# The opening of a Fourier filter and feed-forward kernel: another order for its loads, folds and turns

## The chip, the cores and the metric

The kernel runs on one core of one Trainium2 chip. The core has five engines that work side by side, each in the order of its own instruction list: TensorE (PE, with PEld for its weight loads), VectorE (DVE), ScalarE (ACT), GpSimd (POOL) and SyncE (SP, which only issues DMAs). Transfers run on 16 DMA engines; here SP and POOL issue them. The metric is the time of one execution on the device in microseconds (us). The kernel before takes 904.9 us, the median of 3 runs (904.34 to 905.48).

## The reference

Two stages follow one another. The first filters each of 256 columns along a sequence of 3008 in the frequency domain; the second is a feed-forward block with a normalisation ahead of it.

```python
def _attn_ref(x, filt_r, filt_i):          # x: 8 x 3008 x 256
    X = np.fft.rfft(x, axis=1)
    Y = X * (filt_r + 1j * filt_i)[None, :, :]
    return np.fft.irfft(Y, n=x.shape[1], axis=1)

def _moe_ref(x, w_gate, w_val, w_out, rms_g):   # x: 24064 x 256, w: 256 x 1536
    rms = np.sqrt(np.mean(x * x, axis=-1, keepdims=True) + 1e-06)
    xn = x / rms * rms_g
    g = xn @ w_gate
    silu = g * (1.0 / (1.0 + np.exp(-g)))
    return silu * (xn @ w_val) @ w_out
```

## The kernel before

The transforms of length 3008 = 47 x 64 are done as matmuls with constant tables, in three steps for each of the eight batches:

- s1: a transform of length 47 (`s1`, L139, one matmul for two of 32 row groups, 16 calls a batch; psum name psa). Its result goes to DRAM (`a_tmp`, one store for four calls) and comes back in another layout in four reads (`load_a2`, L156).
- s2 and s2z: the transform of length 64 (`s2`, psp), the product with the filter, and the way back (`s2z`, psz), 12 calls a batch. The result goes to DRAM (`z_tmp`, one store for three calls) and comes back in another layout (`load_z2`, L240). I call this the z trip.
- s3: the way back over 47 (`s3`, L247, psy), 16 calls a batch, with the sums of squares taken on ScalarE, rho = 1/rms on GpSimd (`s3r`) and the scaling on VectorE (`s3n`). The result goes to DRAM (`n_tmp`) and comes back transposed as `xn`.

The feed-forward block runs in chunks of up to 512 tokens. A unit (`unit`, L337) is one of 12 blocks of 128 of the 1536 inner columns: two matmuls for the gate (pg), two for the value (pv), Silu on ScalarE (sg), the product on VectorE (hh). Its projection (`project`, L354, po) follows three units later (LAG). A chunk's result is copied out of PSUM by ScalarE and VectorE and stored. Batch 0 makes 8 chunks of 376 tokens, every other batch 6; units are counted on through all chunks, so that unit 12 begins the second chunk of batch 0 and unit 96 the first of batch 1.

The order is written by hand (`manual_schedule`): each engine gets its instructions in the order of the calls. From the first unit on, `plan` holds lists of steps by slot: `at(k, f, ...)` puts a step behind the matmuls of unit k, and within a slot s3n, then s3r, then s2z, then all others run (`ORDER`, L430). So batch 0's remaining chunks (from the third, `PRE` = 2), batch 1's s2 and s3 and all of the later batches run between units.

The opening (L492 to L551) is what comes before the first unit. Batch 0 is worked through s1, s2 and s2z without a trip between s1 and s2. Near its end, at j = 10 of the loop at L513, GpSimd issues the four loads of batch 1's x (`load_x(1)`, which cast and so are issued by GpSimd), folds four of the twelve weight stages (`fold_w`: weights times the norm's gain, into their final type) and issues the first third of w_out (`load_wo`). After the last s2z the z trip's reads are issued, with eight rows each of 32 (`load_z2(0, 0, 8)`, `load_z2(0, 8, 8)`), and four more weight stages (`load_w(4)`). Then come 12 of batch 1's 16 s1 calls, s3 of the first two chunks, the last four s1 calls, and the two chunks' scaling and turn: `turn_n` (L294) scales a chunk (`s3n_first`), turns it with eight matmuls (psn) and copies it to `xn`, one half by ScalarE and one by VectorE. Four folds stand between the two turns, four in slot 5.

Buffers that matter: the x tiles, the a tiles have four each; `xn` and the weight stages share nine; PSUM has eight banks; `z2` and `a2` have one buffer each.

Of the kernel before, what the change touches and what calls it, by code (L numbers as in the profile page):

```python
# [74 lines left out]
def kernel(  # L75
# [11 lines left out]
    nc = tc.nc  # L87
# [8 lines left out]
    a_dram = nc.dram_tensor("a_tmp", (B, NS, 4, RP, D), FP16, kind="Internal").ap()  # L96
# [8 lines left out]
    def bank(name):  # L105
        return psum.tile([P, 512], FP32, tag="bank", name=name)
# [15 lines left out]
    PRE = 2  # L122
# [4 lines left out]
    st = [Batch() for _ in range(B)]  # L127


    def load_x(b):  # L130
        v = st[b]
        v.x = []
        for g in range(4):
            xt = work.tile([PX, 8, D], FP16, tag="xt", name="xt", bufs=4)
            nc.gpsimd.dma_start(
                xt, x[b].rearrange("(p r) d -> p r d", r=RP)[:, ds(8 * g, 8), :])
            v.x.append(xt)

    def s1(b, i, eng):  # L139
        v = st[b]  # L140
        if i % 4 == 0:
            v.a = work.tile([QZ, 8, D], FP16, tag="a_sb", name="a_sb", bufs=4)
        ps = bank("psa")
        nc.tensor.matmul(ps[0:QZ, :], w1_sb, v.x[i // 4][:, ds(2 * (i % 4), 2), :],  # L144
                         start=True, stop=True)
        dst = v.a[:, ds(2 * (i % 4), 2), :]
        src = ps[0:QZ, :].rearrange("p (r d) -> p r d", r=2)
        if eng == 0:
            nc.scalar.activation(out=dst, in_=src, func=AXT.Copy)  # L149
        else:  # L150
            nc.vector.tensor_copy(out=dst, in_=src)
        if i % 4 == 3:
            nc.sync.dma_start(
                a_dram[b].rearrange("s c r d -> (s c) r d")[:, ds(8 * (i // 4), 8), :], v.a)

    def load_a2(b):  # L156
        v = st[b]
        v.a2 = work.tile([P, NS, D], FP16, tag="a2", name="a2", bufs=1)
        for cr in range(4):
            nc.sync.dma_start(v.a2[cr:P:4], a_dram[b, :, cr].rearrange("s r d -> r s d"))  # L160
# [79 lines left out]
    def load_z2(b, r0=0, n=RP):  # L240
        v = st[b]
        if r0 == 0:
            v.z2 = work.tile([QZ, RP, D], FP16, tag="z2", name="z2", bufs=1)
        nc.sync.dma_start(v.z2[:, ds(r0, n), :],
                          z_dram[b, ds(r0, n)].rearrange("r c s d -> (c s) r d"))
# [36 lines left out]
    def s3n_first(c):  # L282
        v = st[0]
        n = work.tile([PY, 8, D], FP16, tag="n_sb", name="n0", bufs=2)
        for k in range(2):
            ps, rho = v.y.pop(2 * c + k)
            nc.vector.tensor_tensor(out=n[:, ts(k, 2), :],
                                    in0=ps[0:PY, :].rearrange("p (r d) -> p r d", r=2),
                                    in1=rho.unsqueeze(-1).to_broadcast([PY, 2, D]), op=ALU.mult)
        if c >= PRE:  # L290
            nc.sync.dma_start(n0_dram[c], n[:, 0:4, :])
        return n

    def turn_n(c):  # L294
        n = s3n_first(c)
        xn = work.tile([P, 2, 512], FP16, tag="xn", name="xn", bufs=9)
        for dh in range(2):
            ps = bank("psn")
            for r in range(4):
                nc.tensor.matmul(ps[:, ts(r, PY)], n[:, r, ts(dh, P)], eye_sb[0:PY, 0:PY],  # L300
                                 start=(r == 0), stop=(r == 3))
            dst = xn[:, dh, 0:4 * PY].rearrange("d (p r) -> d r p", r=4)
            src = ps[:, 0:4 * PY].rearrange("d (r p) -> d r p", r=4)
            if dh == 0:
                nc.scalar.activation(out=dst, in_=src, func=AXT.Copy)
            else:
                nc.vector.tensor_copy(out=dst, in_=src)
        st[0].xn[c] = xn
# [12 lines left out]
        st[b].xn[c] = xn  # L321

    for v in st:
        v.t12, v.y, v.xn = {}, {}, {}


    chunks = []
# [69 lines left out]
    def at(slot, f, *args):  # L397
        plan.setdefault(slot, []).append((f, args))

    for c in range(PRE, RP // 4):  # L400
        k = 2 + 8 * (c - PRE)
        at(k, s3, 0, 2 * c, 2)
        at(k + 1, s3, 0, 2 * c + 1, 2)
        at(k + 2, s3r, 0, 2 * c, 2)
        at(k + 4, s3n_first, c)
        at(k + 7, load_xn_first, c)

    for b in range(1, B):
        end = FIRST + UNITS * (b - 1)
        o_s1 = 44 if b == 2 else end - 118  # L410
        o_s2, p_s2 = (12, 3) if b == 1 else (end - 75, 2)
        o_s3 = 62 if b == 1 else end - 31
        if b > 1:
            at(o_s1 - 18, load_x, b)
            for i in range(16):
                at(o_s1 + i, s1, b, i, i % 2 if b == 2 else 0)
            at(o_s1 + 16, load_a2, b)
        for j in range(12):
            k = o_s2 + p_s2 * j
            at(k, s2, b, j)  # L420
            at(k + (3 if b < 2 else 5), s2z, b, j)
        at(k + (4 if b < 2 else 6), load_z2, b)
        for q in range(16):
            k = o_s3 + q + (q // 2 if b == 1 else q // 4)
            at(k, s3, b, q)
            at(k + 1, s3r, b, q)
            at(k + 2, s3n, b, q)
        for c in range(6):
            at(k + 3 + c, load_xn, b, c)
# [46 lines left out]
    def load_w(n):  # L476
        for w_d, w_sb, dt_, k in pieces[len(stages):len(stages) + n]:
            stage = work.tile([P, 512], FP32, tag="xn", name="stage", bufs=9)
            nc.sync.dma_start(stage, w_d[ds(dt_ * P, P), ts(k, 512)])
            stages.append(stage)  # L480

    def fold_w(i, eng):
        w_d, w_sb, dt_, k = pieces[i]
        eng.tensor_scalar(out=w_sb[:, dt_, ts(k, 512)].rearrange("a (i p) -> a i p", i=4),  # L484
                          in0=stages[i].rearrange("a (p i) -> a i p", i=4),
                          scalar1=g_sb[:, ds(dt_, 1)], scalar2=None, op0=ALU.mult)

    def load_wo(k):
        nc.gpsimd.dma_start(wo_sb[:, ts(k, 4), :],
                            moe_w_out.rearrange("(k p i) d -> k p i d", p=P, i=4)[k])  # L490

    with tc.manual_schedule():  # L492
        load_x(0)
        nc.sync.dma_start(w1_sb, w1_d)
        nc.sync.dma_start(u_sb, u_d)
        nc.sync.dma_start(eye_sb, eye_d)
        nc.sync.dma_start(w0_sb, w0_d)
        nc.sync.dma_start(t_sb, t_d)
        for dh in range(2):
            nc.sync.dma_start(g_sb[:, ds(dh, 1)], moe_rms_g[ds(dh * P, P)].unsqueeze(-1))  # L500
        nc.vector.memset(half_sb, -0.5)
        load_f(0, nc.gpsimd)
        for g in range(4):
            s1_first(g)
            if g < 3:
                make_v(2 * g)
                make_v(2 * g + 1)
            if g > 0:

                nc.vector.memset(fr_sb[0:1, 6 * g, 0:1], 0.0)  # L510
                load_f(g, nc.sync)
        copy_f(0)
        for j in range(15):  # L513
            if j < 12:
                turn(j)
            if 0 <= j - 2 < 12:
                s2(0, j - 2)
            if j in (2, 5, 8):
                copy_f(j // 3 + 1)
            if 0 <= j - 4 < 12:  # L520
                s2z(0, j - 4)
            if j == 6:
                load_w(4)
            if j == 10:
                load_x(1)
                for i in range(4):
                    fold_w(i, nc.gpsimd)
                load_wo(0)
        s2z(0, 11)
        load_z2(0, 0, 8)  # L530
        load_z2(0, 8, 8)
        load_w(4)
        for i in range(12):
            s1(1, i, i % 2)
        for c in range(PRE):
            s3(0, 2 * c, 2)
            s3(0, 2 * c + 1, 2)
            s3r(0, 2 * c, 2)
        for i in range(12, 16):
            s1(1, i, 1)  # L540
        load_wo(1)
        load_wo(2)
        turn_n(0)
        load_w(4)
        for i in range(4, 8):
            fold_w(i, nc.vector)
        turn_n(1)
        load_z2(0, 16, 16)
        load_a2(1)
        for i in range(8, 12):  # L550
            at(5, fold_w, i, nc.vector)  # L551

        total = len(chunks) * JT
        for u in range(total + LAG):
            if u < total:
                unit(u // JT, u % JT)
                steps(u)
            if u >= LAG:
                project((u - LAG) // JT, (u - LAG) % JT)
        assert not plan, sorted(plan)  # L560
# [30 lines left out]
```

## Time and profile before

| | us |
|---|---|
| median of 3 runs | 904.9 |
| the profiled execution's own time | 903.57 |
| its span in the profile | 901.7 |
| TensorE busy in the span | 862.3 |
| VectorE busy | 645.6 |
| ScalarE busy | 640.1 |
| GpSimd busy | 336.5 |
| first s3 matmul of batch 0 | 49.28 |
| first unit | 60.97 |
| first s3 matmul of batch 1 | 138.23 |
| first unit of batch 1 (unit 96) | 175.31 |

The page cuts the span into 40 slices of 22.5 us and gives each a digit of busy tenths. A row of the chain of waits is a piece of the chain that ended last: its start, its length, and the instruction or transfer. A row of the timeline gives start, length, engine, line, operation, result<-operands, shapes, and in brackets the idle time before it with what ended it. A row of the windows gives a stretch, its length, the busy time of PE, PEld, DVE, ACT and POOL with the number of instructions, the granted TensorE clock, the DMA share and GB/s.

### The profile page before, as it was taken

How to read it: one execution, taken by the hardware profiler on the slowest of the kernel's cores; microseconds unless marked ns; L12 is line 12 of the kernel's file. 1: busy time of each engine (PE TensorE's matmuls, PEld its weight loads, DVE VectorE, ACT ScalarE, POOL GpSimd, SP SyncE). 2: the span in 40 equal slices, each digit the busy share in tenths (PEclk: the TensorE clock that was granted, in tenths of full speed). 3: DMA queues.
4: the chain of work that ended last, by engine and by line, in shares of the span. 5: the costliest groups of instructions: out<-in, count | busy, mean ns of one | idle time of the engine just before them, and what ended most of it. 6: DMA issues, size and time to landing. Idle time of an engine off the chain costs nothing.

```text
span 901.7 us, 16399 instructions
## 1 busy us (share of the span) xinstructions
PE 862.3 (96%) x5528; PEld 549.6 (61%) x5528; DVE 645.6 (72%) x1025; ACT 640.1 (71%) x1455; POOL 336.5 (37%) x438
## 2 busy tenths in 40 slices
PE   5659999999999999999999999999999999999997
PEld 4326766666556655666556665566656665665655
DVE  4658887895588947697477965789477985865554
ACT  5546678777886778677886878867786775854543
POOL 3712104592245803285044821459033850500000
PEclk9859999999999999999999999999999999999999
DMA  9995766565436565354645554365653425260101
GB/s 211 238 257 124 167 156 212 122 145 130 144 101 143 128 146 170 99 108 129 163 146 129 138 123 151 106 131 145 146 159 100 97 78 117 77 130 24 42 29 45
DMA packets 140796, 117.30 MB, mean 130 GB/s; under 512 B 53960, under 2 KB 125256, under 8 KB 140712
## 3 DMA queue, kind: packets, MB, share of 16 engines
q1 hardware_dynamic: 136472, 102.36, 42.5%
q0 software_dynamic: 4240, 13.90, 8.6%
q8 instruction: 43, 0.70, 0.3%
q14 instruction: 41, 0.34, 0.1%
HBM read 56.96 MB, written 60.42 MB: 130 GB/s over the span
## 4 chain that ended last, share of the span: by engine, by line
PE 87%; ACT 4%; DMA 3%; DVE 2%; issue 2%; POOL 1%; ACTq 0%; SPq 0%; DVEq 0%; POOLq 0%
PE po L364 26%; PE pv L346 26%; PE pg L342 25%; PE psy L250 2%; PE psa L144 2%; ACT junk L256 2%; PE psz L229 2%; PE psp L200 2%; ACT sg L349 2%; DMA fi_sb<-in_filt_i_dram 1%; DMA z_tmp<-z_sb 1%; DMA z<-z_tmp 1%; DVE t L208 1%; DVE hh L351 0%; POOL fi_sb L450 0%
## 5 line engine op out<-in xcount | busy, mean ns | idle before, releaser
L351 DVE TENSOR_TENSOR hh<-pv,sg 128x512 f16<-128x512 f32 (+2 forms) x600 | 392.5, 658 | 219.8 <-ACT sg L349 128.3
L349 ACT ACTIVATE sg<-pg 128x512 f32<-128x512 f32 (+2 forms) x600 | 340.6, 568 | 193.8 <-PE pg L342 159.9
L364 PE MATMUL po<-wo_sb,hh 128*128 128x256 f16 (+2 forms) x2304 | 349.4, 272 | 0.2 <-DVE n_sb L276 0.2
L346 PE MATMUL pv<-xn,wv_sb 128*128 128x512 f16 (+2 forms) x1200 | 342.2, 367 | 4.4 <-ACT sg L349 3.8
L342 PE MATMUL pg<-xn,wg_sb 128*128 128x512 f16 (+2 forms) x1200 | 342.4, 367 | 0.6 <-DVE wg_sb L484 0.3
L364 PEld LDWEIGHTS <-hh 128*128 128x128 f16 (+2 forms) x2304 | 235.0, 104 | 102.4 <-DVE n_sb L276 0.5
L346 PEld LDWEIGHTS <-wv_sb 128*128 128x128 f16 x1200 | 117.5, 98 | 132.7 <-issue 6.3
L265 POOL TENSOR_SCALAR me<-ms 96x2 f32<-96x2 f32 (+1 forms) x120 | 26.0, 217 | 349.3 <-ACT junk L256 348.4
L342 PEld LDWEIGHTS <-wg_sb 128*128 128x128 f16 x1200 | 117.4, 98 | 14.1 <-issue 1.1
L217 POOL TENSOR_TENSOR pi<-pi,fi_sb 64x512 f32<-64x512 f32 x72 | 91.3, 1268 | 70.4 <-ACT pi L214 66.6
L256 ACT ACTIVATE junk<-psy 96x256 f16<-96x256 f32 x256 | 97.1, 379 | 20.9 <-PE psy L250 8.7
L218 POOL TENSOR_TENSOR qq<-pr,pi 128x512 f16<-128x512 f32 x72 | 91.6, 1272 | 10.2 <-DVE pi L216 4.4
L267 POOL TENSOR_TENSOR rho<-me,half_sb 96x2 f32<-96x2 f32 (+1 forms) x120 | 87.3, 728 | 10.0
L276 DVE TENSOR_TENSOR n_sb<-psy,rho 96x512 f16<-96x512 f32 x112 | 75.8, 677 | 0.0
L234 ACT ACTIVATE z_sb<-psz 128x512 f16<-128x512 f32 x96 | 57.3, 597 | 10.1 <-PE psz L232 5.8
L149 ACT ACTIVATE a_sb<-psa 96x512 f16<-96x512 f32 x94 | 55.4, 591 | 7.2 <-PE psa L144 3.5
L250 PE MATMUL psy<-z,t_sb 96*96 96x512 f16 x128 | 49.2, 389 | 7.8 <-DMA z<-z_tmp 7.8
L216 DVE TENSOR_TENSOR pi<-psp,fi_sb 64x512 f32<-64x512 f32 x72 | 49.9, 693 | 1.9
L215 DVE TENSOR_TENSOR pr<-psp,fr_sb 128x512 f32<-128x512 f32 x72 | 49.6, 689 | 0.6
L256 ACT ACTIVATION_READ_ACCUMULATOR junk<-psy 96x1 f32 x256 | 49.0, 191 | 0.0
L214 ACT ACTIVATE pi<-psp 64x512 f32<-64x512 f32 x72 | 42.4, 588 | 6.1
L144 PE MATMUL psa<-xt,w_sb 94*96 94x512 f16 x112 | 42.5, 399 | 3.0 <-DMA xt<-in_x_dram 2.8
(53 smaller groups left out, 382.6 us busy)
## 6 DMA issues: line engine op xcount, KB each, us to landing
out_dram<-o SPq DMA_DIRECT2D x70, 256.0 KB, 2.5
z_tmp<-z_sb SPq DMA_DIRECT2D x32, 384.0 KB, 2.3
xt<-in_x_dram POOLq DMA_DIRECT2D x32, 376.0 KB, 7.3
a_tmp<-a_sb SPq DMA_DIRECT2D x28, 384.0 KB, 3.6
a<-a_tmp SPq DMA_DIRECT2D x28, 384.0 KB, 5.5
z<-z_tmp SPq DMA_DIRECT2D x7, 1536.0 KB, 10.0
n_tmp<-n_sb SPq DMA_DIRECT2D x28, 384.0 KB, 3.0
out_dram<-o SPq DMA_DIRECT2D x14, 224.0 KB, 2.6
```

What stands on the lines that cost most here:

```text
L144: nc.tensor.matmul(ps[0:QZ, :], w1_sb, v.x[i // 4][:, ds(2 * (i % 4), 2), :], start=True, stop=True)
L217: nc.gpsimd.tensor_tensor(out=pi[64:P], in0=pi[64:P], in1=fi[64:P], op=ALU.mult)
L218: nc.gpsimd.tensor_tensor(out=qq, in0=pr, in1=pi, op=ALU.subtract)
L250: nc.tensor.matmul(ps[0:PY, :], t_sb, v.z2[:, ts(q, 2), :], start=True, stop=True)
L256: nc.scalar.activation(out=junk, in_=ps[0:PY, ts(i, D)], func=AXT.Square, scale=0.0625, accum_out=v.ms[:, ds(k + i, 1)])
L267: nc.gpsimd.tensor_tensor(out=rho, in0=me, in1=half_sb[:, 0:2 * pair], op=ALU.pow)
L276: nc.vector.tensor_tensor(out=v.n[:, ds(2 * (q % 4), 2), :], in0=ps[0:PY, :].rearrange("p (r d) -> p r d", r=2), in1=rho.unsqueeze(-1).to_ ...
L342: nc.tensor.matmul(pg[:, 0:w], wg_sb[:, dt_, ts(jt, P)], xn[:, dt_, 0:w], start=(dt_ == 0), stop=(dt_ == 1))
L346: nc.tensor.matmul(pv[:, 0:w], wv_sb[:, dt_, ts(jt, P)], xn[:, dt_, 0:w], start=(dt_ == 0), stop=(dt_ == 1))
L349: nc.scalar.activation(out=sg[:, 0:w], in_=pg[:, 0:w], func=AXT.Silu)
L351: nc.vector.tensor_tensor(out=hh[:, 0:w], in0=pv[:, 0:w], in1=sg[:, 0:w], op=ALU.mult)
L364: nc.tensor.matmul(po[0:n, ts(s4 % 2, D)], hh[:, ds(s4 * wb, n)], wo_sb[:, jt, :], start=(jt == 0 and s4 % 2 == 0), stop=(jt == JT - 1 and ...
```

## The change

The diff is shown whole. It does the following:

- `load_x` takes a list of groups, and batch 1's four groups are loaded in three steps on GpSimd's list: groups 0 and 1, two folds, group 2, two folds, group 3, then the first third of w_out.
- The first two z reads take four rows each instead of eight; rows 8 to 15 are read later, rows 16 to 31 in slot 4, behind the reads of batch 1's a.
- `s1` can hand its stores back (`later`). Only eight s1 calls of batch 1 stand before s3 now, four more stand between s3 of the first and of the second chunk, all on VectorE; the last four are in slots 2 to 4, on ScalarE. The first two a stores follow after s3, then the z read of rows 8 to 15, the last four weight stages, the third a store; the fourth a store and the a reads are in slot 4.
- `turn_n` gets its scaled chunk from outside. Both chunks are scaled before the units, the first is turned there, the second in slot 2.
- The eight folds on VectorE are in slots 0, 1, 4 and 5, two in each.
- In the plan, batch 0's third and later chunks and batch 1's s2 and s2z come four slots later, batch 1's s3 one slot later.

```diff
--- before.py
+++ after.py
@@ -127,16 +127,15 @@
     st = [Batch() for _ in range(B)]
 
 
-    def load_x(b):
-        v = st[b]
-        v.x = []
-        for g in range(4):
+    def load_x(b, groups=range(4)):
+        v = st[b]
+        for g in groups:
             xt = work.tile([PX, 8, D], FP16, tag="xt", name="xt", bufs=4)
             nc.gpsimd.dma_start(
                 xt, x[b].rearrange("(p r) d -> p r d", r=RP)[:, ds(8 * g, 8), :])
             v.x.append(xt)
 
-    def s1(b, i, eng):
+    def s1(b, i, eng, later=None):
         v = st[b]
         if i % 4 == 0:
             v.a = work.tile([QZ, 8, D], FP16, tag="a_sb", name="a_sb", bufs=4)
@@ -150,8 +149,13 @@
         else:
             nc.vector.tensor_copy(out=dst, in_=src)
         if i % 4 == 3:
-            nc.sync.dma_start(
-                a_dram[b].rearrange("s c r d -> (s c) r d")[:, ds(8 * (i // 4), 8), :], v.a)
+            def store(a=v.a):
+                nc.sync.dma_start(
+                    a_dram[b].rearrange("s c r d -> (s c) r d")[:, ds(8 * (i // 4), 8), :], a)
+            if later is None:
+                store()
+            else:
+                later.append(store)
 
     def load_a2(b):
         v = st[b]
@@ -291,8 +295,7 @@
             nc.sync.dma_start(n0_dram[c], n[:, 0:4, :])
         return n
 
-    def turn_n(c):
-        n = s3n_first(c)
+    def turn_n(c, n):
         xn = work.tile([P, 2, 512], FP16, tag="xn", name="xn", bufs=9)
         for dh in range(2):
             ps = bank("psn")
@@ -321,7 +324,7 @@
         st[b].xn[c] = xn
 
     for v in st:
-        v.t12, v.y, v.xn = {}, {}, {}
+        v.x, v.t12, v.y, v.xn = [], {}, {}, {}
 
 
     chunks = []
@@ -398,7 +401,7 @@
         plan.setdefault(slot, []).append((f, args))
 
     for c in range(PRE, RP // 4):
-        k = 2 + 8 * (c - PRE)
+        k = 6 + 8 * (c - PRE)
         at(k, s3, 0, 2 * c, 2)
         at(k + 1, s3, 0, 2 * c + 1, 2)
         at(k + 2, s3r, 0, 2 * c, 2)
@@ -408,8 +411,8 @@
     for b in range(1, B):
         end = FIRST + UNITS * (b - 1)
         o_s1 = 44 if b == 2 else end - 118
-        o_s2, p_s2 = (12, 3) if b == 1 else (end - 75, 2)
-        o_s3 = 62 if b == 1 else end - 31
+        o_s2, p_s2 = (16, 3) if b == 1 else (end - 75, 2)
+        o_s3 = 63 if b == 1 else end - 31
         if b > 1:
             at(o_s1 - 18, load_x, b)
             for i in range(16):
@@ -522,33 +525,45 @@
             if j == 6:
                 load_w(4)
             if j == 10:
-                load_x(1)
-                for i in range(4):
-                    fold_w(i, nc.gpsimd)
-                load_wo(0)
+                load_x(1, (0, 1))
+                fold_w(0, nc.gpsimd)
+                fold_w(1, nc.gpsimd)
         s2z(0, 11)
-        load_z2(0, 0, 8)
-        load_z2(0, 8, 8)
+        load_x(1, (2,))
+        fold_w(2, nc.gpsimd)
+        fold_w(3, nc.gpsimd)
+        load_x(1, (3,))
+        load_wo(0)
+        load_z2(0, 0, 4)
+        load_z2(0, 4, 4)
         load_w(4)
-        for i in range(12):
-            s1(1, i, i % 2)
+        a_stores = []
+        for i in range(8):
+            s1(1, i, i % 2, a_stores)
         for c in range(PRE):
             s3(0, 2 * c, 2)
             s3(0, 2 * c + 1, 2)
             s3r(0, 2 * c, 2)
-        for i in range(12, 16):
-            s1(1, i, 1)
+            if c == 0:
+                for i in range(8, 12):
+                    s1(1, i, 1, a_stores)
+        for f in a_stores[:2]:
+            f()
+        load_z2(0, 8, 8)
+        load_w(4)
+        a_stores[2]()
         load_wo(1)
         load_wo(2)
-        turn_n(0)
-        load_w(4)
-        for i in range(4, 8):
-            fold_w(i, nc.vector)
-        turn_n(1)
-        load_z2(0, 16, 16)
-        load_a2(1)
-        for i in range(8, 12):
-            at(5, fold_w, i, nc.vector)
+        n0 = s3n_first(0)
+        turn_n(0, n0)
+        n1 = s3n_first(1)
+        at(2, turn_n, 1, n1)
+        for i in range(4, 12):
+            at((0, 0, 1, 1, 4, 4, 5, 5)[i - 4], fold_w, i, nc.vector)
+        for i in range(12, 16):
+            at(2 + (i - 11) // 2, s1, 1, i, 0)
+        at(4, load_a2, 1)
+        at(4, load_z2, 0, 16, 16)
 
         total = len(chunks) * JT
         for u in range(total + LAG):
```

## The prediction

> **What bounds the kernel now.** I read the page first, then the chain of waits of the opening, the timeline there, and the timeline around the first place where a later batch leans on the opening. The two strips of the page's second part:
>
> ```profile
> PEclk9859999999999999999999999999999999999999
> DMA  9995766565436565354645554365653425260101
> ```
>
> TensorE is at 9 tenths from the fourth slice on, and the waits after 75 us put only 5 us of TensorE idle time down to anything. So the time is the opening's length plus a nearly full TensorE stream: what counts is how early the feed-forward units start, and holes made later. Only in the first slices is the DMA at 9 while TensorE is not, and TensorE runs there at half clock. The chain of waits of the first 120 us, start and length:
>
> ```profile
> 35.32 7.07 DMA z_tmp<-z_sb
> 42.94 6.29 DMA z<-z_tmp
> 49.28 0.64 PE psy L250
> ...
> 58.02 0.66 DVE wg_sb L484
> 58.68 0.58 DVE wv_sb L484
> 59.26 1.20 DVE n L287 x2
> 60.51 0.66 PE psn L300 x6
> 61.17 0.63 PE pg L342 x2
> ```
>
> The last z store and the first z read are 13.4 us in which TensorE has nothing but four matmuls of s1; then 11.7 us of normalising and turning both chunks, with four folds between, before the first unit (its first matmul at 60.97). I call the first s3 matmul T: 49.28 before. What shares the DMA, by the timeline:
>
> ```profile
> 29.86 2.10 POOL L135 DMA_DIRECT2D xt<-in_x_dram  x4
> 32.12 2.07 POOL L484 TENSOR_SCALAR wg_sb<-stage,g_sb 128x512 f16<-128x512 f32 x1 [0.15 <-issue]
> 40.20 0.62 POOL L489 DMA_DIRECT2D wo_sb<-in_moe_w_out_dram  x1
> 42.55 1.13 SPq L244 DMA_DIRECT2D z<-z_tmp  x2
> 58.04 10.97 SPq L160 DMA_DIRECT2D a<-a_tmp  x4
> ```
>
> The four x loads land 5.2, 6.7, 8.5 and 10.7 us after their issues (35.05, 37.05, 39.4, 42.1): one group per 2.35 us. The last z store, issued with groups two to four still moving, lands after 7.1; the first, issued at 24.70 before them, after 3.5.
>
> **The change, part by part. (1) x in three steps.** POOL issues groups 0 and 1 (29.86 plus two issues of 0.53), folds twice (2.04 each), issues group 2 at 35.0, folds twice, issues group 3 at 39.6 and the first wo load at 40.2, as before. The last z store still shares with group 2, but not with group 3: 7.1 - 2.35 = 4.75, landing at 40.05 instead of 42.4. Gain 2.35; bounds 0 and 3.6 (down to 3.5). s1 of groups 0 to 2 stays hidden under the trip; group 3 lands at some 44, ten us before its matmuls among the units.
>
> **(2) The first read halved.** 192 instead of 384 KB before T. A 1536 KB read of this kind lands in a median 10.0 us, so 192 KB is worth about 1.0. Against it, group 3 is now issued just when the read is: a whole group is 2.35, nothing is the other end. I take 0.8, as the two queues take turns and the wo load was beside the read before too. So T' = 49.28 - 2.35 - 1.0 + 0.8 = 46.7, gain 2.55 (bounds 0 and 4.9).
>
> The Trainium skill (DMA: Bandwidth & Descriptors, Queues, rings and completion order) says each DMA engine goes round-robin, packet by packet, between the queues with work; by that rule alone group 3 takes its whole 2.35 out of the read, T' is 48.3, and the sum below loses 1.5. The 7.1 against 3.5 of the z stores agrees with sharing.
>
> **(3) Order from T' to the first unit.** ScalarE squares from T+0.66 at 0.50 each; the first rho is ready at T+4.1 (52.32 plus 1.05). On VectorE four s1 casts (2.48) end at T'+4.0, hidden by that; two n (1.27) to 5.4; the turn's eight matmuls to 6.1; the copy (1.01) to 7.1. The first unit is at T'+6.9, against T+11.7: four folds, the other n pair and the second turn no longer stand before it. That is not all gain, since they come back among the units. TensorE to the start of unit 8: 6.9, three units at half clock (two pairs of 0.63 each: 3.8), the second turn 0.65, four s1 matmuls 1.2 (0.22 to 0.43 each), five units at 0.97 (0.64 and a projection 0.33) 4.85, two psy 0.45, half a unit more at low clock 0.6: T'+18.4. VectorE to its last fold: 7.1, n 1.3, first hh at 9.2, then eight folds at 0.59, five hh at 0.5, one copy 1.0: 17.4, just inside. Before, unit 8 waited for the folds until 69.90, T+20.6. Gain 2.2; bounds 0.5 (a clock window more at half rate) and 3.0. Opening: 2.55 + 2.2 = 4.75.
>
> **(4) SP's queue.** The a stores, the weight stages, the second z read and the a2 reads stand behind one another. The last four weights go out after the second z read, near 48 to 52, and landings of 4.1 to 7.9 put them before their folds at some T'+15 to 17. The last a store now waits for s1 15 in slot 4, so the a2 reads are issued near T'+15.5+3.5 = 65.7, and the z read of rows 16 to 31, the n store of the third chunk and its transposed read queue behind them. s2 of the second batch has moved to slot 16, at unit 8 plus 9.7, 74.8. 1536 KB of such packets takes 8 to 10: landing 73.7 to 75.7. I take no stall; bounds 0 and 6.7 (rival C). The third chunk's xn is needed near 85, some 5 us after it lands.
>
> **(5) The second batch's z trip.** s2 and s2z shift by four slots, s3 by one (62 to 63): three slots less for the trip. Before:
>
> ```profile
> 121.65 0.27 PE L229 MATMUL psz<-t,v_sb 128*128 128x256 f16 x1
> 122.91 0.41 SPq L237 DMA_DIRECT2D z_tmp<-z_sb  x1
> 127.03 0.32 SPq L244 DMA_DIRECT2D z<-z_tmp  x1
> 138.23 0.38 PE L250 MATMUL psy<-z,t_sb 96*96 96x512 f16 x1
> ```
>
> The read issued at 127.03 lands by the 10.0 median at 137.0: 1.2 us spare of the 16.6 between psz and psy. In the new slots the same span on TensorE is the psz themselves (0.45), eight slots with s1 (1.185 apart) and three without (0.97), 12.85: 3.7 less. Stall 3.7 - 1.2 = 2.5. SP now has the out stores of a chunk (2.2 to 3.1 for three) ahead of the z store, worth 0 to 1.6; on the other side, VectorE's extra casts in slots 44 to 52 may make these slots longer. I leave both at nothing; bounds 0.4 and 4.1. Behind the waiting psy stand all units: nothing covers it.
>
> **(6) The n trip to unit 96** is a slot shorter too. Before, the transposed read was issued at 171.11, lands after 3.5, and unit 96 starts at 175.31: 0.7 spare, a slot is 0.97, so 0.3 lost, of which I count 0 to 1.0; I take 0.1, since a stall at 63 moves both.
>
> **Sum.** 4.75 - 2.5 - 0.1 = 2.15 us, say 2.2. The profiled execution's 903.6 (span 901.7) becomes 901.4, and the median of 904.9, 1.3 above it, becomes 902.7.
>
> **A clock price on the hole.** The windows view:
>
> ```profile
> 15.50:18.90 3.40, 1.77 (x28) 1.37 (x27) 2.93 (x8) 1.80 (x5) 0.93 (x1) 1.00 0.98 235
> 18.90:22.30 3.40, 3.40 (x23) 2.80 (x23) 2.87 (x5) 2.37 (x5) 2.63 (x2) 0.50 1.07 242
> ```
>
> A stretch of 3.4 us with TensorE busy for 1.77 was followed by one at clock 0.50. A hole of 2.5 us inside one such stretch would cost half of the next: 1.7 more. Split over two stretches it would leave each over 60% busy, and 28 to 35.3 us, with 5.03 of 7.30 busy, kept 1.00. I price it at nothing in the forecast and as rival B.
>
> The Trainium skill (TensorE: Matmul & The Clock Gate, Part 1) has the clock fall after an idle window of about 3.4 us; by it a 2.5 us hole is free and the sum stands, by the row above the sum is 0.5. The trace's drop at 18.9 without such an idle window speaks for the row.
>
> **Rivals.** *A, the forecast:* 902.7, own range 900 to 903.1. *B, the gain is paid back:* the hole at slot 63 draws a slow clock stretch (1.7), or group 3 and the wo load take the whole of the halved read (1.55). Either leaves 0.5: 904.4. For it: the row at 15.5, and the DMA strip at 9. Against: the phase of the clock is open, and the read is short. *C, slower:* the a2 reads. Before, their four issues took 10.97 us and the last landed 15.9 after the first issue (67.4 plus 6.5 against 58.04). Nothing now moves until the last a store has landed, so if they took 15.9 again, they would land at 81.6 and slot 16 would wait 6.7: 2.2 - 6.7 = 4.5 slower, 909.4. It makes the kernel slower beyond 0.2% once the stall passes 4.0. For it: the a2 wait sits in TensorE's order, and the DMA is at 9 until 72 us. Against: then a 768 KB z read was ahead of them (landing after 12.3), now behind; and the next batch's four issues took 3.19. *D, the z trip is hidden:* if the units around slots 44 to 60 run slower in VectorE, or the read lands at 9 rather than 10, most of the 2.5 is not lost twice: 904.9 - 4.6 = 900.3, and with the high end of T' 898.
>
> **How the numbers follow.** A 0.38, B 0.28, C 0.21, D 0.13. 0.2% is 1.8 us, about what this measurement can tell from no change. A and D are faster, 0.51; a little of C lands inside the band, and so with B 0.28 same and 0.21 slower. The range runs from D's deep end, 898.5, to inside C, 907.5: below it lies hardly anything, above it half of C.
>
> **What would show it.** Step 1: the last z store lands near 40. Step 2: the first psy near 46.7; at 48.3 or later, group 3 took the read. Step 3: the first unit some 7 us after psy, unit 8 some 18.4. Step 4: no TensorE wait at the first psp; a wait there is C. Step 5: TensorE idle some 2.5 us before the first psy of batch 1, ended by the z read; none is D, a clock of 0.50 behind it is B. Step 6: a wait of under 1 us before unit 96. The forecast is wrong if psy is not earlier than before, or if the holes after 75 us exceed the opening's gain.

## The result, and the profile after

The changed kernel takes 908.61 us, the median of 5 runs (907.05 to 909.15), against 904.9 for the kernel before, run beside it (5 runs, 903.54 to 906.08). The ratio is 1.0036, with a 95% interval of 1.0021 to 1.0052: it is slower, by 3.7 us at the medians and by 1.9 to 4.7 by the interval. The profiled execution took 909.15, the longest of its runs, with a span of 907.3; that of the kernel before, at 903.57 with a span of 901.7, lies below its median. So the two traces are 5.6 us apart, and show more loss than the medians.

The two strips of the page of the changed kernel, the granted clock and the DMA share in 40 slices of 22.7 us:

```profile
PEclk9869998999999999999999999999999999999999
DMA  8977766365545555255644554465543425260111
```

The DMA digits of the opening are 8, 9, 7 where they were 9, 9, 9, and the clock strip has an 8 in the seventh slice, 136 to 159 us, that the kernel before didn't have. The lead and its loss follow from the start of each unit on TensorE, changed kernel minus before:

| unit | changed minus before, us |
|---|---|
| 0 | -5.95 |
| 8 | -3.09 |
| 24 | -4.12 |
| 48 | -4.01 |
| 60 | -2.45 |
| 64 | +1.55 |
| 66 | +3.61 |
| 90 | +4.08 |
| 96 | +5.62 |
| 599 (the last) | +5.62 |

So the lead is 3.1 us at unit 8 and 4.1 at unit 24. Not all of the 4.1 is gained: the second batch's s2 and s2z now come four slots later, and between units 8 and 24 the changed kernel has 6 psp and 8 psz matmuls in its trace where the kernel before has 8 and 12. They start 0.11 us apart, so the six are some 0.65 us of work put off. They come back between units 48 and 60 (2 and 8 against none and 4), where s2 shares the slots with the third batch's s1 and 1.6 of the lead goes; 0.45 of that is TensorE idle, and the rest is not traced further.

Then 6.1 go between units 60 and 66, where s3 of the second batch begins, 0.5 up to unit 90 (one of the three psy matmuls that had stood between units 60 and 66 now comes behind them), and 1.5 at unit 96. From there on the two kernels run alike.

The chain of waits of the changed kernel, start and length of each piece:

```profile
35.92 6.44 DMA z_tmp<-z_sb
42.91 5.12 DMA z<-z_tmp
48.05 0.65 PE psy L254
...
53.95 1.03 ACT xn L308
55.02 0.78 PE pg L345 x2
...
130.67 10.05 DMA z<-z_tmp
140.76 0.66 PE psy L254
...
173.48 3.98 DMA n_tmp<-n_sb
177.47 3.41 DMA xn<-n_tmp
```

The last z store lands at 42.4, as before, though the x loads had been put around it. The first psy is at 48.05 instead of 49.28, the first unit 7.0 us later instead of 11.7. Then the chain leaves TensorE twice more: for the second batch's z read, which ends at psy 140.76 (before 138.23), and for the last n store and its transposed read ahead of unit 96. TensorE's waits between 30 and 902 us, in total, number and longest, the first row from the kernel before:

```profile
PE psy L250 <- DMA z<-z_tmp: 7.8, 1, 7.8
...
PE psy L254 <- DMA z<-z_tmp: 12.3, 2, 8.4
...
PE psa L143 <- DMA xt<-in_x_dram: 2.3, 2, 1.5
...
PE pg L345 <- DMA xn<-n_tmp: 1.4, 1, 1.4
```

The 12.3 are 8.4 in the opening and 3.85 before the first psy of batch 1. Around that second hole, the windows view with the borders set where the granted clock changes; the columns are the stretch, its length, busy PE, PEld, DVE, ACT and POOL, clock, DMA share, GB/s:

```profile
135.83:139.24 3.41, 1.08 (x8) 0.55 (x6) 1.67 (x4) 1.18 (x3) 0.00 (x0) 1.00 1.19 209
139.24:142.65 3.41, 1.89 (x7) 1.15 (x8) 0.00 (x0) 0.94 (x4) 0.13 (x1) 0.50 0.78 255
142.65:146.07 3.42, 3.42 (x15) 1.99 (x12) 0.87 (x2) 1.91 (x6) 1.73 (x4) 0.50 0.45 125
```

A stretch with TensorE busy for 1.08 of 3.41 us was followed by one at half clock; in that one the hole still left only 1.89 busy, and a second one at half clock followed. That is how a hole of 3.85 became a loss of 6.1. SyncE's issues on the way to it (start, length, line, transfer), and TensorE at its end:

```profile
123.24 0.32 SPq L295 DMA_DIRECT2D n_tmp<-n  x1
123.66 2.25 SPq L384 DMA_DIRECT2D out_dram<-o  x3
125.97 0.53 SPq L153 DMA_DIRECT2D a_tmp<-a_sb  x1
126.60 0.36 SPq L241 DMA_DIRECT2D z_tmp<-z_sb  x1
...
140.76 0.66 PE L254 MATMUL psy<-z,t_sb 96*96 96x512 f16 x1 [3.85 <-DMA z<-z_tmp]
```

The copy that fills the z store's tile ended at 125.18; the store left at 126.60, behind the three out stores of a chunk and an a store of the third batch.

### The profile page after: what moved, and what is told of

Its sections match the earlier page's. It is cut to its first block, busy times and chain, and to the rows that moved or that the text cites. A ratio compares the mean times of both kernels' runs of the same rounds, so it can differ in the third digit from the quotient of the medians.

```text
span 907.3 us, 16400 instructions
## 1 busy us (share of the span) xinstructions
PE 866.0 (95%) x5528; PEld 551.5 (61%) x5528; DVE 645.0 (71%) x1023; ACT 641.6 (71%) x1457; POOL 336.6 (37%) x438
## 4 chain that ended last, share of the span: by engine, by line
PE 85%; DMA 5%; ACT 4%; issue 2%; DVE 2%; POOL 1%; SPq 0%; ACTq 0%; DVEq 0%; POOLq 0%
PE po L367 26%; PE pv L349 25%; PE pg L345 25%; PE psy L254 2%; PE psa L143 2%; ACT junk L260 2%; PE psz L233 2%; PE psp L204 2%; DMA z<-z_tmp 2%; ACT sg L352 2%; DMA xt<-in_x_dram 1%; DMA z_tmp<-z_sb 1%; DVE t L212 1%; DMA fr_sb<-in_filt_r_dram 1%; DMA n_tmp<-n_sb 0%
## 5 line engine op out<-in xcount | busy, mean ns | idle before, releaser
L254 PE MATMUL psy<-z,t_sb 96*96 96x512 f16 x128 | 49.9, 393 | 12.3 <-DMA z<-z_tmp 12.3
L218 ACT ACTIVATE pi<-psp 64x512 f32<-64x512 f32 x72 | 42.4, 588 | 6.4 <-PE psp L204 0.4
```

The lines of the kernel that those rows point to most:

```text
L254: nc.tensor.matmul(ps[0:PY, :], t_sb, v.z2[:, ts(q, 2), :], start=True, stop=True)
```

## The experiments

Ratios are against the kernel before, run beside each kernel on the same chip. "Lead" is how much earlier a unit starts than the same unit before. Where two variants were not run side by side, the difference of their ratios is the fairer comparison: 0.001 is 0.9 us.

**1. s3 of the second batch four slots later.** Theory Z, in the expectations: the shorter z trip makes the loss. Theory W: the new slots themselves cost it.

```diff
-        o_s3 = 63 if b == 1 else end - 31
+        o_s3 = 67 if b == 1 else end - 31
```

> The changed kernel with batch 1's s3 in slot 67 instead of 63. Theory Z (two trips): the loss sits in batch 1's z trip (a hole of 3.9 us before its first psy, then 6.8 us at half clock, together some 6.2) and in its n trip (1.4 before unit 96). Four slots later the z hole is under 0.5 and the clock stays at 1.00, but the n trip loses four slots, so the wait before unit 96 grows from 1.4 to 5 or 6 and may draw a slow clock stretch itself: 906 to 909 us. Theory W (the rival: the opening gained nothing, its lead of 4 us is work put off, and the loss is spread over the denser slots 44 to 56): taking the hole away gives nothing, the n trip costs more: 911 to 913.

Measured 910.49 (907.7 to 911.03), ratio 1.0066 (1.0051 to 1.0081). The hole is gone: only the opening's wait for a z read is left, and unit 66 keeps a lead of 4.05. But 5.0 us go between units 66 and 90, 3.7 more at unit 96, which s3 now ends closer to, and 2.9 behind it. TensorE's waits in this run, SyncE's issues, and ScalarE ahead of the 2.7:

```profile
PE psy L254 <- DMA z<-z_tmp: 8.2, 1, 8.2
...
PE pg L345 <- ACT sg L352: 3.7, 4, 2.7
PE pg L345 <- DMA xn<-n_tmp: 3.6, 1, 3.6
...
141.66 3.09 SPq L164 DMA_DIRECT2D a<-a_tmp  x4
144.85 2.94 SPq L384 DMA_DIRECT2D out_dram<-o  x3
...
151.44 0.38 ACT L381 ACTIVATE o<-po 128x256 f32<-128x256 f32 x1 [2.07 <-DMA out_dram<-o]
```

Both the 2.7 and the 3.6 are followed by half clock (from 151.66 and 178.97), and the lead of 4.05 has become a delay of 7.52 by the end. The 3.6 is the n trip. The 2.7, at 152.25, is another road: a chunk's out stores stand behind the third batch's a reads on SyncE, the copy of the next chunk waits 2.07 for one of them, and the Silu that TensorE waits for stands behind this copy. So s3 is held by the z trip ahead of it and the n trip behind it, and moving it alone also meets a queue that had been harmless. By its time this run fits neither theory cleanly (it lies between the two forecasts), by its place it fits Z.

**2. s2 a little denser, s3 a slot earlier.** The trip gets its slots back where it starts.

```diff
-        o_s2, p_s2 = (16, 3) if b == 1 else (end - 75, 2)
-        o_s3 = 63 if b == 1 else end - 31
+        o_s2, p_s2 = (16, 8 / 3) if b == 1 else (end - 75, 2)
+        o_s3 = 62 if b == 1 else end - 31
...
-            k = o_s2 + p_s2 * j
+            k = int(o_s2 + p_s2 * j + 0.01)
```

> The changed kernel with batch 1's twelve s2 every 8/3 slots instead of every 3 (from slot 16, so that the last s2z is back in slot 48) and its s3 back in slot 62: the z trip and the n trip have their old lengths in slots, and the opening is the changed one. Theory Z: no TensorE wait over 0.5 us at the first psy of batch 1 or at unit 96, clock 1.00 there, and what the opening gained is left: 901 to 903 us. Theory W: 905 to 908, the lead gone by unit 60.

Measured 899.11 (898.63 to 899.23), ratio 0.9945 (0.9933 to 0.9958): faster than both kernels, and below the forecasts of both theories. TensorE's waits for the z and x transfers:

```profile
PE psy L254 <- DMA z<-z_tmp: 8.5, 1, 8.5
...
PE psa L143 <- DMA xt<-in_x_dram: 2.0, 2, 1.3
```

One wait for a z read is left, the opening's; no wait for `xn` is left. The lead is 4.42 at unit 8, 5.20 at 48, 4.70 at 60, and stays at 4.7 to the end. The opening is the changed kernel's, so its gain was there all along, and the later plan had thrown it away. Theory W falls as the main cause: s2 starts at the same slot 16, and of the 1.6 lost between units 48 and 60 only 0.5 is left. Part of the lead at unit 8 is the phase of the clock: in this execution TensorE ran at half clock from 40.42 to 57.49, 17.07 us, in the changed kernel's for 20.48.

**3. The later plan alone,** on the kernel before.

```diff
-        k = 2 + 8 * (c - PRE)
+        k = 6 + 8 * (c - PRE)
...
-        o_s2, p_s2 = (12, 3) if b == 1 else (end - 75, 2)
-        o_s3 = 62 if b == 1 else end - 31
+        o_s2, p_s2 = (16, 3) if b == 1 else (end - 75, 2)
+        o_s3 = 63 if b == 1 else end - 31
```

> The kernel before with the three plan numbers of the change alone (batch 0's later chunks from slot 6, batch 1's s2 from slot 16, its s3 from slot 63); the opening is the old one. Theory Z: both holes appear without the opening's gain: the wait before psy 3 to 4 us, a slow clock stretch or two behind it, over 1 us before unit 96: 910 to 914 us. Theory W: the plan is harmless, 904 to 906.

Measured 914.75 (912.86 to 914.92), ratio 1.0115 (1.0101 to 1.0128). TensorE's waits:

```profile
PE psy L250 <- DMA z<-z_tmp: 11.0, 2, 6.2
...
PE pg L342 <- DMA xn<-n_tmp: 1.5, 1, 1.5
```

Without the new opening the same two holes come, 4.8 before psy of batch 1 (11.0 less the opening's 6.2) and 1.5 at unit 96, again with two stretches at half clock behind the first; the z hole is longer than the 3 to 4 us that theory Z had expected. Unit 66 is 7.16 late, the end 9.28. The plan's part of the change costs 9 us in this execution, the shortest of its four, and 10.4 by the ratio. The opening part repairs 3.7 of it by the two traces and 7.1 by the ratios; the changed kernel's trace is of its longest execution.

**4. The hole filled, not removed.** 20 matmuls whose result nobody reads are put into slot 62; the outputs are the same.

```diff
+    def fill(n):
+        ps = bank("fill")
+        for k in range(n):
+            nc.tensor.matmul(ps, wg_sb[:, 0, 0:P], wv_sb[:, 0, 0:512],
+                             start=(k == 0), stop=(k == n - 1))
...
+    at(62, fill, 20)
```

> The changed kernel with 20 matmuls of 128x512 (0.22 us each at full clock, some 4.3 in all, results not read) in slot 62, where TensorE else waits for the z read. If the slow clock behind the hole is a price of its own (theory Z): the clock stays at 1.00 after the first psy of batch 1 and the time falls by 2 to 2.8, to 906 us; the z read lands when it did. If the units behind the hole are slow for another reason, the time stays at 908 to 909.

Measured 905.28 (901.26 to 907.34, 11 runs), ratio 1.0013 (1.0001 to 1.0025). The psy comes no earlier, at 140.69, and TensorE does no more useful work, but the clock stays up:

```profile
135.80:139.20 3.40, 3.40 (x17) 1.57 (x16) 0.55 (x1) 0.00 (x0) 0.00 (x0) 1.00 1.23 217
139.20:142.60 3.40, 3.40 (x25) 2.17 (x23) 1.33 (x4) 2.33 (x8) 0.35 (x2) 1.00 0.58 217
```

With the hole filled, the loss from unit 60 to 66 is 3.75 instead of 6.06. So 2.3 of it was the slow clock. The ratios differ by 2.1, the medians by 3.3.

The next four start from experiment 2, where nothing later covers what the opening does, and take one of its parts out each. One trace of each can't carry a small difference: with the same opening, the lead at unit 8 is 3.1 in the changed kernel and 3.5 to 4.4 in experiments 1, 2, 4, 9 and 10, and 4.4 is experiment 2. From some 40 us on TensorE ran at half clock for 17.07 us there, for 20.48 in experiment 5 and for 23.89 in 6 to 8. So I give the ratios beside the traces.

**5. x in one step.** All four groups are issued together, the folds after them.

```diff
             if j == 10:
-                load_x(1, (0, 1))
+                load_x(1)
                 fold_w(0, nc.gpsimd)
...
-        load_x(1, (2,))
         fold_w(2, nc.gpsimd)
         fold_w(3, nc.gpsimd)
-        load_x(1, (3,))
         load_wo(0)
```

> The version with s2 every 8/3 slots (899.1 us), but all four x groups of batch 1 issued at once, as before the change, then four folds. If the steps carry the opening's gain as predicted (step 1: 2.35 us on the last z store): first psy 2 us later than 47.65 and 901 to 902 us. If the gain is in the order after psy (step 3), and the third step only moves the same traffic onto the z read: first psy within 1 us, 898.5 to 900 us.

Measured 899.44 (899.15 to 900.23), ratio 0.9951 (0.9938 to 0.9965), 0.3 above experiment 2 with ranges that overlap. The pieces of the chain of waits, of experiment 2 first:

```profile
35.80 6.53 DMA z_tmp<-z_sb
42.49 5.03 DMA z<-z_tmp
...
35.55 7.89 DMA z_tmp<-z_sb
43.61 3.75 DMA z<-z_tmp
```

The store is 1.4 us longer than the 6.53 of experiment 2, the read 1.3 shorter than its 5.03, and the first psy is at 47.49 against 47.65. What the steps take out of the store, they put into the read.

**6. The third step behind psy.** The fourth group and the w_out third are issued after the first chunk's s3.

```diff
-        load_x(1, (3,))
-        load_wo(0)
         load_z2(0, 0, 4)
...
             if c == 0:
+                load_x(1, (3,))
+                load_wo(0)
                 for i in range(8, 12):
```

> The version with s2 every 8/3 slots, but the last x group and the first third of w_out are issued only behind the first chunk's rho on GpSimd, after the first z read has landed. The trace of the changed kernel has the z read's packets start only when both of these are done. If they hold the read: its landing falls from 5.4 us to some 3, the first psy comes 2 to 3 us earlier (45), and the time falls to 896.5 to 898. If the read is held by something else (its own small packets, the x group before): first psy within 0.7 us of 47.65 and 899 us; a late x group would then show as a TensorE wait at s1 12 and 900 to 902 us.

Measured 899.53 (897.92 to 900.26), ratio 0.9945 (0.9933 to 0.9958). Its chain:

```profile
42.17 2.80 DMA z<-z_tmp
...
49.18 7.96 DMA xt<-in_x_dram
...
67.50 8.54 DMA a<-a_tmp
```

The read takes 2.80 instead of 5.03; psy comes at 45.10 and the first unit at 52.07, both 2.55 us earlier, 2.2 of it in the read. That is the price of sharing the DMA with the third step. Yet the time is not the 896.5 to 898 that was expected with it, and by unit 8 the kernel is 0.3 behind experiment 2: s1 waits 0.54 for the late group, and TensorE runs at half clock until 60.96 instead of 57.49, which can be up to 1.7 of it (an estimate, half of the 3.47). Then the first psp waits 1.6 for the reads of batch 1's a, whose last landed at 76.04 against 73.56. The chain now runs through the transfers that had been hidden.

**7. Both turns and four folds before the units,** as in the kernel before.

```diff
-        at(2, turn_n, 1, n1)
-        for i in range(4, 12):
-            at((0, 0, 1, 1, 4, 4, 5, 5)[i - 4], fold_w, i, nc.vector)
+        for i in range(4, 8):
+            fold_w(i, nc.vector)
+        turn_n(1, n1)
+        for i in range(8, 12):
+            at(5, fold_w, i, nc.vector)
```

> The version with s2 every 8/3 slots, but four folds and the second chunk's turn stand before the first unit again, the other four folds in slot 5, as before the change. By the prediction's step 3 (2.2 us at unit 8) the first unit is some 4 us later and the time 901 to 902 us. If the order of turns and folds is neutral, because the units behind it wait for the same folds: 898.5 to 900 us.

Measured 901.16 (900.2 to 902.51), ratio 0.9968 (0.9955 to 0.998). Unit 8 is 1.28 later and the last unit 1.39 than in experiment 2, though psy came 0.37 earlier. The first unit is 1.46 later, not 4, and the ratios differ by 2.1: the new order is worth 1.4 to 2.1.

**8. The first read whole.**

```diff
-        load_z2(0, 0, 4)
-        load_z2(0, 4, 4)
+        load_z2(0, 0, 8)
```

> The version with s2 every 8/3 slots, but one z read of eight rows in place of two of four ahead of s3. By the prediction's step 2 the halved read is worth 1.0 us: first psy 0.7 to 1.3 us later, 899.8 to 900.4. If the read is held by what is queued beside it and not by its own size: within 0.4 us, 898.7 to 899.5.

Measured 901.34 (900.21 to 901.58), ratio 0.9966 (0.9954 to 0.9979). The first psy is 1.47 later, unit 8 2.07, the last unit 2.42, and the ratios differ by 1.9: the halved read is worth 1.5 to 2.4, more than the 0.7 to 1.3 expected.

**9. The second batch's last z store from ScalarE.** The last two runs go back to the changed kernel, and ask whether the stores ahead on SyncE made the hole longer.

```diff
         if j % 3 == 2:
-            nc.sync.dma_start(
+            q = nc.scalar if (b, j) == (1, 11) else nc.sync
+            q.dma_start(
```

> The changed kernel, with one edit: the second batch's last z store is issued by ScalarE, right behind the copy that fills it, not by SyncE behind a chunk's three out stores and an a store. Theory S (the stores ahead of it on SyncE make the hole 1.4 us longer than I had reckoned): the z store goes out near 125.2 instead of 126.60, the read near 129.3, and TensorE's wait before the second batch's first psy is 2.4 to 2.6 us instead of 3.85; the clock may still fall behind it, so the time is 1.4 to 4 us below the changed kernel's 908.6: 904.6 to 907.2. Rival R (the transfers themselves are late, because out stores and z store share the DMA engines): the store lands as late as before, the wait stays above 3.4, and the time is 907.5 to 909.

Measured 904.12 (903.12 to 905.96, 10 runs), ratio 0.9998 (0.9988 to 1.0008). The store, the read that waits for it and TensorE's hole, by the timeline:

```profile
124.84 0.34 ACTq L242 DMA_DIRECT2D z_tmp<-z_sb  x1
...
128.13 0.51 SPq L249 DMA_DIRECT2D z<-z_tmp  x1
...
138.49 0.42 PE L255 MATMUL psy<-z,t_sb 96*96 96x512 f16 x1 [1.94 <-DMA z<-z_tmp]
```

The hole shrinks from 3.85 to 1.94, below the 2.4 to 2.6 that theory S gave: the store leaves as soon as its copy ends, not 1.4 later, and it also lands 2.71 after its issue instead of 4.01, so that the read follows it by 3.3 instead of 4.1. The clock holds. The windows, with the borders of this run's clock:

```profile
133.76:137.17 3.41, 2.79 (x21) 1.73 (x18) 2.54 (x7) 1.93 (x5) 0.00 (x0) 1.00 1.19 219
137.17:140.58 3.41, 2.09 (x15) 1.46 (x16) 0.58 (x2) 1.61 (x7) 0.50 (x2) 1.00 0.52 204
140.58:143.99 3.41, 3.41 (x25) 2.41 (x24) 2.72 (x6) 3.08 (x12) 1.94 (x5) 1.00 0.53 151
```

The hole is split over two stretches that stay 2.79 and 2.09 busy. Between units 60 and 66 the loss is 1.57 instead of 6.06, and the time falls by 3.4 us by the ratios, 4.5 by the medians, for one store on another queue. Theory S holds for the queue's 1.4. R, that the store would land as late as before, falls; but why it lands in 2.71 here is not shown, as it took 4.0 in the kernel before too, where no out stores stood ahead of it.

**10. The last n store from ScalarE too.**

```diff
         if q % 4 == 3:
-            nc.sync.dma_start(n_dram[b, :, ds(8 * (q // 4), 8), :], v.n)
+            eng = nc.scalar if (b, q) == (1, 15) else nc.sync
+            eng.dma_start(n_dram[b, :, ds(8 * (q // 4), 8), :], v.n)
```

> As the run before it, and the second batch's last n store is issued by ScalarE too. Theory S (the store leaves 0.3 us late behind the out stores and takes 1.0 longer to issue because SyncE still works on them): TensorE's wait before unit 96 falls from 1.4 us to 0.1 to 0.6, and the time is about 1 us below the run before it. Rival R (the last scaling on VectorE, 0.5 us later, and the landing of store and transposed read make the wait): the wait stays at 0.9 to 1.4, and the time is within 0.5 us of the run before it.

Measured 905.07 (903.0 to 906.23, 10 runs), ratio 1.0004 (0.9995 to 1.0013). TensorE ahead of unit 96, and ScalarE behind the store:

```profile
169.12 1.64 ACT L354 ACTIVATE sg<-pg 128x376 f32<-128x376 f32 x4 [2.70 <-PE pg L347]
...
175.43 0.60 PE L347 MATMUL pg<-xn,wg_sb 128*128 128x512 f16 x2 [0.30 <-ACT pi L218]
```

The wait before unit 96, 1.37 in the changed kernel and 0.89 in experiment 9, is down to 0.30, as theory S said. The profile puts it down to ScalarE; the read of `xn` landed only 0.05 before it ended. The time is not the 1 us better that S forecast. From unit 90 to 96 this execution loses 0.58 where the one before lost 1.05, but its hole before psy is 2.56 against 1.94, which takes that back. ScalarE did nothing for 2.70 us around its store, with the Silu of four units behind it; that cost the stream only 0.1. The hole was longer because the z read took 10.90 us from issue to landing here and 10.31 there. Why it did, and whether the medians, 0.95 apart with ranges that overlap, really differ, is open.

## Why the prediction was wrong

The forecast was 902.7 in a range of 898.5 to 907.5; 908.6 is beyond it. Its account of the places was right: the opening gains, and two trips farther on pay it back. Its last sign of being wrong is what came true: the holes after 75 us exceed the opening's gain. The sum failed in step 5 above all. By the two traces it is 7.8 off, 2.15 gained against 5.62 lost: 3.6 in step 5, 1.4 in step 6, 1.7 in the opening, 0.6 between units 8 and 60, and 0.5 up to unit 90.

**(5) The second batch's z trip** is the step that failed. It took a hole of 2.5 and nothing for the out stores and the clock: 2.5 in all. The trace has 6.1 between units 60 and 66. Two terms that had been named and set to nothing were not nothing. SyncE's queue held the z store for 1.4 of the 0 to 1.6 allowed; without it, by subtraction, the hole of 3.85 would be 2.4, so the 2.5 was sound. The slots had been counted rightly: from psz to psy, without the wait, TensorE took 12.96 for the 12.85 forecast. And the hole at 3.85 pulled the clock down for two stretches, not one: 2.3 by the trace of experiment 4, 2.1 by its ratio. The prediction's own row, a stretch with 1.77 busy and half clock behind it, had shown this, and was kept for rival B at 1.7. The clock's price is not the queue's doing alone: the hole began at 136.91, so a hole of 2.4 would have left the stretch that ended at 139.24 just as idle, and the first slow stretch would probably have come all the same. What the queue's 1.4 added is the part of the hole in the second. Moving the one store took off 3.4 (by the ratios) of what the changed kernel lost; how much of that is the phase of the clock is open, since experiment 9 has one trace.

**(6) The n trip** took 0.1 of the allowed 0 to 1.0; the wait was 1.4 and unit 96 lost 1.5. The lost slot is no more than was counted: from the last psy to unit 96 the stream without its wait is 11.1 us, against 11.7 before: 0.6 less, and a whole slot is 0.97. What was not counted is that the trip itself grew: the last scaling ends 4.8 after its psy instead of 4.1, behind two copies of an out chunk on VectorE, and its store left behind that chunk's three out stores, which before went after it; from there to the first transposed read it took 4.0 instead of 3.4. With the store off SyncE, experiment 10 has 0.30 left of the 0.89 in experiment 9: its place there made most of it.

**(1) x in three steps** took 2.35; it is worth 0 to 0.5 (experiment 5; the end of its span is 0.49 later). The last z store landed at 42.4 as before. The loads were issued at 30.85, a microsecond later than before, and group 2 still went out beside the store. More important, what the store is spared the read gets: both are on the path, one behind the other.

**(2) The halved read** took 1.0, less 0.8 for group 3. The halving is worth 1.5 to 2.4 (experiment 8), and group 3 with the w_out third cost 2.55 (experiment 6). T' came at 48.05, not 46.7. Of the predicted gain of 2.55 in (1) and (2), 1.23 came. The Trainium skill (DMA: Bandwidth & Descriptors, Queues, rings and completion order) has the engines take turns packet by packet between queues, and the sum made with it, 48.3, was the better one. The turns themselves don't show: in the packet records no packet of SyncE's queue starts between 42.53, when the read was issued on it, and 45.75. By then GpSimd's load of group 3, issued at 40.80, had landed (45.58), and that of w_out, issued at 41.34, was near its end (46.98). In experiment 6, with neither in flight, the read's packets start 0.9 after its issue.

**(3) The order from psy to the first units** took 2.2 and measured 1.4 to 2.1 (experiment 7). The first unit came 7.0 after psy where 6.9 was forecast, unit 8 at 18.1 where 18.4 was. The opening in all gave 3.1 by unit 8, and 3.5 to 4.4 in the five other traces with the same opening, for the 4.75 forecast. 1.3 of the lack is T', and 0.6 a reading: the kernel before was counted from 69.90, the second gate matmul of its unit 8, which waits for a fold, while its first starts at 69.27. So the terms erred in both directions.

**(4) SyncE's queue and the a reads:** no stall was taken, and none came. The reads went out at 66.46 and landed by 74.5, and the first psp ran at 75.54 without a wait. Rival C, the one slower case, fell with that. The result was slower by a road that none of the rivals had alone: A's hole, made longer by a queue, with B's clock behind it.

One loss has no term in the sum: slots 48 to 60 took 1.6 of the lead, and 1.6 in experiment 3 too, where s2 and the third batch's s1 meet as they do here, but only 0.5 with the denser s2. Some 0.65 of it is the work put off between units 8 and 24, which had never been gained. The prediction had thought of longer slots there only as cover for the trip.

## What to carry to other kernels

When a step is moved later, follow the transfers that it starts to the next point where TensorE needs them, on the store's way out as well as the read's way in, and count what stands ahead of each store on its issuing queue. Don't price a hole by its length alone: ask what share of the clock's stretch it leaves busy, and where the hole falls in it: here a hole of 1.94 cost 1.6 us, and one of 3.85 cost 6.1. Compare two kernels only at places where they have done the same work. And before a gain in an opening is called lost, take the later part of the change off or mend it: with the denser s2 (experiment 2), the opening left the kernel 4.7 to 5.0 us faster.

## What the runs showed of the hardware

In these traces the granted clock changes only at borders a multiple of 3.41 us apart, and goes by how busy TensorE was in the stretch before, though not by that alone. Half clock followed stretches with 1.08 of 3.41 busy (the changed kernel), 1.30 and 0.82 (experiment 1) and 1.22 (experiment 3). Full clock was kept after 2.09 (experiment 9) and 2.04 (experiment 10). There is no sharp border in between. With the same 2.05 busy in experiment 3 the clock fell once and held once, and it held after 1.85 in experiment 6 and after 1.71 near the end of experiment 5 (891.09 to 894.51):

```profile
33.01:36.43 3.42, 2.05 (x11) 1.02 (x11) 1.68 (x3) 1.88 (x4) 3.42 (x2) 1.00 1.06 188
36.43:39.84 3.41, 2.55 (x7) 0.64 (x4) 2.06 (x3) 1.80 (x4) 3.41 (x3) 0.50 1.02 250
183.20:186.62 3.42, 2.05 (x11) 1.10 (x12) 2.51 (x5) 1.02 (x3) 3.26 (x3) 1.00 0.87 192
186.62:190.03 3.41, 3.41 (x25) 2.29 (x24) 2.95 (x5) 3.03 (x7) 2.27 (x3) 1.00 0.94 189
...
74.61:78.02 3.41, 1.85 (x15) 1.41 (x16) 1.98 (x4) 0.84 (x2) 1.26 (x2) 1.00 0.79 165
78.02:81.44 3.42, 3.42 (x28) 2.61 (x28) 3.04 (x6) 2.05 (x4) 0.00 (x0) 1.00 0.27 62
```

What decides between 1.7 and 2.1 is open. Where a hole falls in the stretches matters beside its length: 2.56 us, split 1.20 to 1.37, left the clock at full in experiment 10. The Trainium skill (TensorE: Matmul & The Clock Gate, Part 1) gives an idle window of about 3.4 us for the fall; the length agrees with these traces, but the window need not be idle: one that was busy for 1.77 of 3.41, in the prediction's row, was not busy enough.

Once down, the clock needed more to come back in these traces than it had needed to stay up. It stayed at half for a second stretch where the first slow one was 1.89 busy (the changed kernel), 0.83 (experiment 3) and 2.42 (experiment 1, behind its second wait), and came back after 2.82 (experiment 1, behind its first). Busy time doesn't decide alone here either: in experiment 9 a stretch at half clock that was busy throughout, 48.43 to 51.85, was followed by another.

A psy 2.55 us earlier bought nothing in experiment 6. The transfers that had been put off to free the read, x and with it the reads of a, came back on the chain as pieces of 7.96 and 8.54 us, and the half clock lasted 3.47 us longer than in experiment 2.
